# Seven unread matmuls instead of nine at the start, and at least two out matmuls behind each burst that holds values

## The chip, the cores and the metric

The kernel runs on one core of one Trainium2 chip. The metric is the device time of one execution in microseconds (us). A core has a matrix engine (PE in the profile; its weight loads stand apart as PEld), a vector engine (DVE), an activation engine (ACT), GpSimd (POOL) and a sync engine (SP). Matmuls write into eight banks of an accumulator memory, from where DVE and ACT read the results. The engines run by themselves and wait for each other by semaphores. Each takes its own instructions in the order in which the program has them, so an instruction that waits holds up everything behind it on its engine.

## The reference

Sigmoid attention over 8 batches, 12 heads, 448 positions and 64 channels, followed by a two-layer network with a SiLU in between:

```python
scores = scale * np.matmul(q, k.transpose(0, 1, 3, 2)) - np.log(S)
attn = 1.0 / (1.0 + np.exp(-scores))
x = np.matmul(attn, v)          # then heads side by side: 3584 rows of 768
h = x @ w_in                    # 768 -> 2048
g = h * (1.0 / (1.0 + np.exp(-h)))
out = g @ w_out                 # 2048 -> 768
```

There is no softmax: each score goes through a sigmoid by itself, so attention needs no sums over a row.

## The kernel before, in words

**Groups and tiles.** A group `g` is one batch with four heads (two pairs); there are 24, three to a batch. Each has seven score tiles. A tile (`scores`, L218) is four matmuls into one double bank `psc` (L225), which work beside each other in the four quarters of the array, and one ACT instruction (L232) that takes the sigmoid of all 896 columns and writes `attnT`. The values of a group (`values`, L240) are 28 matmuls (L256) into `pav`, behind which DVE scales two halves into `xT` (L267).

**Start.** The first q comes by two loads on the SP and ACT queues into a buffer `qs` and is cast to half precision by DVE (columns of the first four chunks, L629) and ACT (the rest, L630). The first two chunks of k come by a POOL load with a cast on the way (L617, L124). PE meanwhile runs `keep_busy(9)` (L675): matmuls of 512 columns on a constant, into a bank that nobody reads. Behind it, in PE's order, stand the first transposes (`pe_transpose`, L676 and L196): eight for the first part of q, two for chunk 0 of k, six for the rest of q, two for chunk 1 of k. DVE and ACT copy them out (L203, L186). The scores of tile 0 need all of q and chunk 0 of k. Then comes a list written by hand (`behind`, L698) of what PE does behind each of the tiles 0 to 23; in it `keep_busy(2)` stands behind tiles 2, 3, 6 and 7.

**Batches 0 and 1.** Bursts of two tiles (`burst`, L740) alternate with the first layer for these batches (`first_h`).

**Stretches m = 0, 1, 2.** Each computes attention for the next two batches (42 tiles) and fills PE with the second layer of the two batches before, the out matmuls of 384 columns (`sets`, `out_set`, L504). That layer is done as a Strassen-like product: seven products of eight matmuls each stand in for eight, with sums by DVE. The 42 tiles go in 18 bursts of 2, 2 and 3 tiles, six times over. A burst that finds a complete group waiting also runs that group's values (L745): a round is the seven tiles of a group, so from the second round on that is the first burst of each round, five in a stretch. In what follows **A** is this burst (two tiles and the values), **B** the next (two tiles), **C** the third (three tiles).

**How many out matmuls follow a burst** is planned (L774 to L789). The planner gives each burst a share of the stretch's PE time by its number of tiles, takes off what it reckons for the burst (200 ns, 200 ns a tile, 1330 ns for values) and fills the rest with out matmuls of 163 ns each, but at least one; the remainder goes on to the next burst. Worked through by its own numbers it gives, in m = 0 and m = 2, 9, 8 and 14 in the first round and then 1, 8 and 14 behind A, B and C of the other five. In m = 1, which has 56 out matmuls more, it gives 3 or 4 behind A, 11 or 12 behind B and 17 or 18 behind C. `rows_if_any` (L591), called behind each burst and again half way through its out matmuls, sends at most one sum and one copy to DVE, and a transposing load to SP.

**Accumulator banks in a stretch.** `banks_for_attention(3)` makes three double banks and two single ones. `two_banks` hands out the doubles in turn, to `psc` and, in these stretches, to `pav` too. So each use waits until the use three before it has been read. In the order A1, A2, values, B1, B2, C1, C2, C3 that is: B1 takes the bank of A1, B2 that of A2, C1 that of the values, C2 that of B1, C3 that of B2, and the next A1, A2 and values those of C1, C2 and C3. The single banks hold the products of the second layer in turn (`one_bank`).

Behind a stretch `h_pair` (L362) computes the first layer of its two batches, again as a Strassen-like product; after m = 2 the second layer of the last two batches ends the kernel.

Of the kernel before, what the change touches and what calls it, by code (L numbers as in the profile page):

```python
# [17 lines left out]
def kernel(  # L18
# [19 lines left out]
    NT_B = NQ * NCH  # L38
# [25 lines left out]
    def banks_for_attention(doubles):  # L64
        psum.close()
        banks.clear()
        bufs_of.update(double=doubles, single=NBANK - 2 * doubles)
        for name, bufs in bufs_of.items():
            taken[name] = 0
            new_pool(name, bufs)  # L70
# [7 lines left out]
    def banks_for_h():  # L78
        doubles = [[2 * i, 2 * i + 1] for i in longest_idle("double")]
        ring[:] = sum(doubles[:-2], [])  # L80
        ring.extend(2 * bufs_of["double"] + i for i in longest_idle("single"))
        ring.extend(sum(doubles[-2:], []))
        psum.close()
        banks.clear()
        new_pool("any", 1)
        for i in range(NBANK):
            banks[i] = banks["any"].tile([P, 512], F32, tag=f"any{i}", name=f"any{i}")

    def one_bank(name):
        if "any" in banks:  # L90
            ring.append(ring.pop(0))
            return banks["any"].tile([P, 512], F32, tag=f"any{ring[-1]}", name=name)
        taken["single"] += 1
        return banks["single"].tile([P, 512], F32, tag="single", name=name)
# [83 lines left out]
    def keep_busy(n):  # L178
        if n == 0:
            return  # L180
        pw = one_bank("pw")
        for _ in range(n):
            nc.tensor.matmul(pw, dummy[:, :P], dummy, start=True, stop=True)
# [4 lines left out]
    def pe_transpose(g, pieces=(("k", 0, 4), ("k", 4, NCH), ("q", 0, 4), ("q", 4, NCH))):  # L188
        if ("k", g) not in qkT:
            new_qkT(g)  # L190
        for name, c0, c1, *copy in pieces:
            dst = qkT[name, g].rearrange("p c t -> p (c t)")
            ptr = one_bank(f"ptr{name}")
            for c in range(c0, c1):
                for j in range(2):
                    nc.tensor.matmul(  # L196
                        ptr[j * D : (j + 1) * D, (c - c0) * P : (c - c0 + 1) * P],
                        flat[name, g][:, j, c, :],
                        ident,
                        start=True,  # L200
                        stop=True,
                    )
            (copy[0] if copy else nc.vector.tensor_copy)(  # L203
                dst[:, c0 * P : c1 * P], ptr[:, : (c1 - c0) * P]
            )
# [12 lines left out]
    def scores(g, ch):  # L218
        attnT[g, ch] = p12.tile([P, 2, S], F16, tag="attnT", name="attnT")
        psc = two_banks("psc")  # L220
        for half in range(2):
            own = slice(half * HP, (half + 1) * HP)
            for j in range(2):
                rows = slice(j * D, (j + 1) * D)
                nc.tensor.matmul(  # L225
                    psc[own, j, :S],
                    qkT["k", g][rows, ch, own],
                    qkT["q", g][rows, :, own],
                    start=True,
                    stop=True,  # L230
                )
        nc.scalar.activation(attnT[g, ch], psc[:, :, :S], AF.Sigmoid, bias=bias_s, scale=QKSCALE)  # L232
# [7 lines left out]
    def values(g, end=NCH):  # L240
        b, iq = divmod(g, NQ)
        if b not in xT:
            assert b < 2 or b - 2 in h_done
            xT[b] = p2.tile([P, NPAIR, S], F16, tag="xT", name="xT")
        pav, done_rounds = part_of.pop(g, None) or (None, 0)
        if pav is None and bufs_of["double"] > 2 and "any" not in banks:
            both = two_banks("pav")
            pav = [both[:, half] for half in range(2)]
        elif pav is None:
            pav = [one_bank("pav") for _ in range(2)]  # L250
        for ch in range(done_rounds, end):
            at = attnT.pop((g, ch))
            for half in range(2):
                own = slice(half * HP, (half + 1) * HP)
                for j in range(2):
                    nc.tensor.matmul(  # L256
                        pav[half][j * D : (j + 1) * D, :S],
                        flat["v", g][own, j, ch, :],
                        at[own, j, :],
                        start=(ch == 0),  # L260
                        stop=(ch == NCH - 1),
                    )
        if end < NCH:
            part_of[g] = pav, end
            return
        for half in range(2):
            nc.vector.tensor_scalar_mul(xT[b][:, half * NQ + iq, :], pav[half][:, :S], SX)  # L267
        if iq == NQ - 1:
            ready.add(b)
# [302 lines left out]
    def sets(m):  # L572
        for g in range(0, NCH - 1, 2):
            step = out_set(
                block(m, g), row_blocks(m, g), block(m, g + 1), row_blocks(m, g + 1)
            )
            for i, ns in enumerate(step):
                if m == 0 and g == 0 and i in (10, 14):
                    next(sums)
                if m == 0 and g == 0 and i in (20, 28, 36, 44):  # L580
                    next(in_sums)
                yield ns
        if m % 2 == 1:
            g = NCH - 1
            yield from out_set(
                kept, row_blocks(m - 1, g), block(m, g), row_blocks(m, g), m == B // 2 - 1
            )
# [3 lines left out]
    def rows_if_any(before, copy):  # L591
        if sums_of_x and next(sums_of_x[0], "end") == "end":
            sums_of_x.pop()
        if later and later[0][0] < before:
            g, name = later.pop(0)
            dma_transpose(g, name, copy)
            if name == "q":
                behind_rows(g, before)
# [68 lines left out]
    def values_if_any():  # L667
        if waiting:
            g = waiting.pop(0)
            values(g)  # L670
            after_values(g)
            return True
        return False

    keep_busy(9)  # L675
    pe_transpose(  # L676
        0, (("q", 0, SPLIT), ("k", 0, 1, act_copy), ("q", SPLIT, NCH, act_copy), ("k", 1, FIRST))
    )
# [61 lines left out]
    def burst(n, size=2):  # L740

        new = units[n : n + size]
        for u in new:
            scores(*u)
        with_values = values_if_any()  # L745
        for g, ch in new:
            if ch == NCH - 1:
                waiting.append(g)
                if 9 <= g + 3 < NQB:
                    later.extend(((g + 3, "k"), (g + 3, "q")))  # L750
        return with_values
# [14 lines left out]
    SWITCH, TILE, VALUES, DENSE = 200, 200, 1330, 163  # L766
    for m in range(B // 2 - 1):
        banks_for_attention(3)
        nc.scalar.activation(warm, bias_s, AF.Sigmoid)
        stream = sets(m)  # L770
        for _ in range(FIRST_DENSE):
            next(stream)

        dense = (3 + m % 2) * 7 * NHC - FIRST_DENSE - ENDING  # L774
        sizes = [2, 2, 3]
        costs = sum(SWITCH + TILE * size for size in sizes) * 2 * NQ + VALUES * (2 * NQ - 1)
        total = dense * DENSE + costs
        own = 2 * NQ * (m + 2)
        left, n = 0.0, 2 * NT_B * (m + 1)
        for size in sizes * (2 * NQ):  # L780
            left += total * size / (2 * NT_B) - SWITCH - TILE * size - VALUES * burst(n, size)
            n += size
            rows_if_any(own, nc.vector.tensor_copy)
            count = max(1, round(left / DENSE))
            left -= count * DENSE
            half = count // 2
            for i in range(count):
                next(stream)
                if i == half:  # L789
                    rows_if_any(own, nc.vector.tensor_copy)  # L790
        assert not sums_of_x
        nc.scalar.activation(warm, bias_s, AF.Silu)
        for _ in stream:
            pass
        (g,) = waiting
        waiting.clear()
        banks_for_h()

        def last_values():
            values(g)  # L800
            after_values(g)
            for _ in x_sums(m + 1, NQ - 1, NQ):
                pass
            nc.gpsimd.tensor_copy(gate, tx[m + 1, 4][:1, NQ - 1, :1])

        for i, _ in enumerate(h_pair(m + 1, last_values)):
            if i % 8 == 7:
                rows_if_any(NQB, nc.gpsimd.tensor_copy)
# [33 lines left out]
```

## Time and profile before

| | us |
|---|---|
| median of 3 runs | 369.35 (368.84 to 369.56) |
| the profiled execution's own time | 369.54 |
| its span, first to last instruction | 367.6 |
| PE busy in the span | 359.3 (98%) |
| DVE, ACT, POOL busy | 251.8 (69%), 250.0 (68%), 77.5 (21%) |

By stage, from a table of the profile by stretches of the span (busy us):

| stretch of the span | what | PE | ACT |
|---|---|---|---|
| 0 to 78 | batches 0 and 1 | 74.2 | 60.0 |
| 78 to 123 | m = 0 | 45.0 | 40.9 |
| 123 to 158 | first layer | 35.0 | 21.6 |
| 158 to 209 | m = 1 | 50.9 | 39.5 |
| 209 to 243 | first layer | 34.0 | 20.7 |
| 243 to 293 | m = 2 | 50.0 | 45.6 |
| 293 to 331 | first layer | 38.0 | 21.2 |
| 331 to 367.6 | last second layer | 32.2 | 0.5 |

The end of a matmul is modelled in these records, and a matmul's record lasts longer than the step to the next one, so a PE that is busy without a gap can still have waited for a while. Such waits are read from the starts. A line of the timeline has the start, the time covered, the engine, the line of the code, the operation, what it writes and reads, its shape and how many were put together; in brackets stands idle time of the engine before it and what ended that.

### The profile page before, as it was taken

The page shows a single profiled execution, that of the slowest core. Times are in us where ns is not written, and L with a number is a line of the kernel's source. Part 1 is how long each engine was busy: PE and PEld are TensorE (multiplying, and loading weights), DVE is VectorE, ACT ScalarE, POOL GpSimd, SP SyncE. Part 2 cuts the span into 40 slices and gives each one's busy share as a digit, 9 for nine tenths or more (in the row PEclk, how much of TensorE's full clock was granted, in tenths as well). Part 3 has the DMA queues.
Part 4 walks back from the last instruction along what each step waited for, and adds up shares of the span by engine and source line. Part 5 has one row for each costly group of instructions (what it writes and reads, how often), then busy time and mean ns, then how long its engine had stood idle before and what let it go on. Part 6 is the DMA issues. An engine that isn't in the chain of part 4 may idle for free. (4 is left out here: it accounts for less than half of the span.)

```text
span 367.6 us, 7594 instructions
## 1 busy us (share of the span) xinstructions
PE 359.3 (98%) x3009; PEld 183.8 (50%) x3009; DVE 251.8 (69%) x458; ACT 250.0 (68%) x339; POOL 77.5 (21%) x116
## 2 busy tenths in 40 slices
PE   7999999999999999999999999999999999999995
PEld 3554445545544555545445555554455555555552
DVE  2565559957756587867665768795756677797763
ACT  5998886479998756687777846679998956640000
POOL 8566521040061172000041047000100000000000
PEclk9999999999999999999999999999999999999999
DMA  8999999987989599007589359922863020003333
GB/s 132 198 204 202 204 203 204 197 115 134 153 114 223 117 135 177 2 0 162 92 168 206 61 128 129 135 24 51 151 113 86 19 71 0 3 0 86 87 86 85
DMA packets 65858, 42.78 MB, mean 116 GB/s; under 512 B 36128, under 2 KB 62496, under 8 KB 65824
## 3 DMA queue, kind: packets, MB, share of 16 engines
q0 software_dynamic: 27072, 22.58, 43.0%
q1 hardware_dynamic: 38320, 19.34, 27.0%
q8 instruction: 23, 0.38, 0.4%
q10 hardware_dynamic: 432, 0.39, 0.3%
q14 instruction: 11, 0.09, 0.1%
HBM read 45.61 MB, written 11.01 MB: 154 GB/s over the span
## 5 line engine op out<-in xcount | busy, mean ns | idle before, releaser
L232 ACT ACTIVATE attnT<-psc,bias_s 128x896 f16<-128x896 f32 x168 | 158.1, 1009 | 21.9 <-PE psc L225 21.6
L504 PEld LDWEIGHTS <-S 128*128 128x128 f16 x448 | 41.3, 98 | 36.5 <-issue 8.1
L225 PE MATMUL psc<-qT,kT 64*64 64x448 f16 x672 | 51.1, 362 | 1.4 <-DVE kT L203 0.5
L267 DVE TENSOR_SCALAR xT<-pav 128x448 f16<-128x448 f32 x48 | 27.7, 619 | 32.5 <-PE pav L256 32.5
L124 POOL DMA_DIRECT2D vf<-in_v_dram x24 | 17.3, 721 | 136.0 <-PE pav L256 118.1
L504 PEld LDWEIGHTS <-gTr 128*128 128x128 f16 x336 | 31.3, 98 | 26.6 <-issue 7.7
L504 PE MATMUL po<-T,S 128*128 128x384 f16 x224 | 42.0, 327 | 0.2
L504 PE MATMUL po<-w_out_sb,gTr 128*128 128x384 f16 x224 | 41.6, 327 | 0.0
L378 PEld LDWEIGHTS <-w_in_sb 128*128 128x128 f16 x288 | 27.9, 98 | 26.7 <-issue 1.1
L504 PE MATMUL po<-w_out_sb,S 128*128 128x384 f16 x224 | 40.8, 326 | 0.0
L256 PE MATMUL pav<-attnT,vf 64*64 64x448 f16 x672 | 38.3, 350 | 0.5 <-DVE gTr L303 0.4
L288 PE MATMUL ph<-xT,w_in_sb 128*128 128x448 f16 x192 | 38.7, 353 | 0.1
L378 PE MATMUL pa<-xT,w_in_sb 128*128 128x448 f16 x144 | 33.1, 353 | 0.0
L225 PEld LDWEIGHTS <-kT 64*64 64x64 f16 x672 | 17.8, 104 | 28.7 <-issue 22.3
L378 PEld LDWEIGHTS <-SI 128*128 128x128 f16 x216 | 21.1, 98 | 20.0 <-issue 0.5
L256 PEld LDWEIGHTS <-vf 64*64 64x64 f16 x672 | 21.0, 107 | 13.3 <-issue 3.8
L288 PEld LDWEIGHTS <-w_in_sb 128*128 128x128 f16 x192 | 17.8, 98 | 19.1 <-issue 3.7
L394 ACT ACTIVATE part<-pa 128x448 f32<-128x448 f32 x24 | 13.1, 544 | 19.2 <-PE pa L378 18.3
L504 PE MATMUL po<-T,gTr 128*128 128x384 f16 x112 | 22.1, 327 | 0.0
L372 ACT ACTIVATE gTr<-pc 128x448 f16<-128x448 f32 x24 | 13.1, 544 | 12.9 <-DVE pc L388 12.5
L388 DVE TENSOR_TENSOR part<-pb,part 128x448 f32<-128x448 f32 x24 | 14.9, 621 | 8.3 <-ACT part L394 5.0
L186 ACT ACTIVATE m<-po 128x384 f32<-128x384 f32 x1 | 0.5, 491 | 27.7 <-PE po L504 27.7
(75 smaller groups left out, 468.2 us busy)
## 6 DMA issues: line engine op xcount, KB each, us to landing
out_dram<-osb SPq DMA_DIRECT2D x52, 192.0 KB, 3.0
vf<-in_v_dram POOLq DMA_DIRECT2D x24, 224.0 KB, 6.5
kf<-in_k_dram POOLq DMA_DIRECT2D x23, 224.0 KB, 6.9
qf<-in_q_dram POOLq DMA_DIRECT2D x23, 224.0 KB, 7.4
w_in_sb<-in_moe_w_in_dram POOLq DMA_DIRECT2D x16, 192.0 KB, 8.1
w_out_sb<-in_moe_w_out_dram POOLq DMA_DIRECT2D x4, 768.0 KB, 14.9
out_dram<-osb SPq DMA_DIRECT2D x6, 96.0 KB, 2.1
kT<-kr SPq DMA_TRANSPOSE x18, 3.5
```

What stands on the lines that cost most here:

```text
L124: nc.gpsimd.dma_start(flat[name, g][:, :, c0:c1].rearrange("p i c d -> p i (c d)"), rows_in(name, g)[:, :, c0 * D : c1 * D],)
L186: nc.scalar.activation(o, i, AF.Copy)
L225: nc.tensor.matmul(psc[own, j, :S], qkT["k", g][rows, ch, own], qkT["q", g][rows, :, own], start=True, stop=True,)
L232: nc.scalar.activation(attnT[g, ch], psc[:, :, :S], AF.Sigmoid, bias=bias_s, scale=QKSCALE)
L256: nc.tensor.matmul(pav[half][j * D : (j + 1) * D, :S], flat["v", g][own, j, ch, :], at[own, j, :], start=(ch == 0), stop=(ch == NCH - 1),)
L267: nc.vector.tensor_scalar_mul(xT[b][:, half * NQ + iq, :], pav[half][:, :S], SX)
L288: nc.tensor.matmul(ph[:, :S], w_in_sb[:, cc, fc * P : (fc + 1) * P], xT[b][:, cc, :], start=(at == 0), stop=(at == NCC - 1),)
L372: nc.scalar.activation(gTr[:, r * NG + i, col + c * S : col + (c + 1) * S], h, AF.Silu, bias=0.0, scale=ISX)
L378: nc.tensor.matmul(to, w[:, n, i * P : (i + 1) * P], x[:, n], start=(start and n == 0), skip_group_check=not start, stop=(n == NQ - 1),)
L388: nc.vector.tensor_add(o, po, x)
L394: nc.scalar.activation(got[i, 1], bank[i, "a"], AF.Copy)
L504: nc.tensor.matmul(po[:, :NO2], a[:, fc, :], w[:, fc, :], start=(fc == 0), stop=(fc == NHC - 1))
```

## The change

```diff
-    keep_busy(9)
+    keep_busy(7)
     pe_transpose(
         0, (("q", 0, SPLIT), ("k", 0, 1, act_copy), ("q", SPLIT, NCH, act_copy), ("k", 1, FIRST))
     )
...
         for size in sizes * (2 * NQ):
-            left += total * size / (2 * NT_B) - SWITCH - TILE * size - VALUES * burst(n, size)
+            with_values = burst(n, size)
+            left += total * size / (2 * NT_B) - SWITCH - TILE * size - VALUES * with_values
             n += size
             rows_if_any(own, nc.vector.tensor_copy)
-            count = max(1, round(left / DENSE))
+            count = max(1 + with_values, round(left / DENSE))
             left -= count * DENSE
             half = count // 2
```

Two of the nine unread matmuls ahead of the first transposes go. In the stretches, the least number of out matmuls behind a burst with values rises from one to two. Worked through, the counts behind A, B and C become 2, 7 and 14 instead of 1, 8 and 14 in the five rounds with values of m = 0 and m = 2; m = 1, with 3 or 4 behind A, stays as it is. So in ten places one out matmul moves from behind burst B to ahead of it. The instructions of DVE, ACT, POOL and SP and their order on these engines stay the same, and PE's lose the two matmuls and their two weight loads.

## The prediction

> **What bounds the kernel now.** I read the busy shares first (PE 98%), then the table by stretches, because both parts of the change sit in single stages.
>
> ```profile
> 78.00:123.00 45.00, 45.00 (x465) 22.76 (x464) 32.10 (x60) 40.89 (x45) 8.83 (x14) 1.00 0.97 147
> 243.00:293.00 50.00, 50.00 (x493) 25.43 (x491) 33.97 (x62) 45.59 (x51) 2.15 (x3) 1.00 0.40 74
> ```
>
> The columns after the length are PE, PEld, DVE, ACT and POOL. In the stretches m = 0 and m = 2 PE has no gap, so whatever lengthens its order there lengthens the kernel; but ACT is at 91% as well, so PE may be waiting on ACT inside its "busy" time. For that I read PE's timeline of one round of m = 0 (A, values, out, B, out, C, out) and ACT's beside it.
>
> ```profile
> 92.69 0.57 PE L225 MATMUL psc<-qT,kT 64*64 64x448 f16 x8
> 93.09 1.49 PE L256 MATMUL pav<-attnT,vf 64*64 64x448 f16 x28
> 94.51 0.34 PE L504 MATMUL po<-w_out_sb,gTr 128*128 128x384 f16 x1
> 94.78 0.74 PE L225 MATMUL psc<-qT,kT 64*64 64x448 f16 x8
> 95.45 0.66 PE L504 MATMUL po<-w_out_sb,gTr 128*128 128x384 f16 x3
> 95.95 0.98 PE L504 MATMUL po<-T,S 128*128 128x384 f16 x5
> 96.86 0.76 PE L225 MATMUL psc<-qT,kT 64*64 64x448 f16 x12
> 97.55 1.96 PE L504 MATMUL po<-T,S 128*128 128x384 f16 x11
> ```
>
> ```profile
> 93.18 1.91 ACT L232 ACTIVATE attnT<-psc,bias_s 128x896 f16<-128x896 f32 x2 [0.27 <-PE psc L225]
> 95.28 1.91 ACT L232 ACTIVATE attnT<-psc,bias_s 128x896 f16<-128x896 f32 x2 [0.19 <-PE psc L225]
> 97.35 2.81 ACT L232 ACTIVATE attnT<-psc,bias_s 128x896 f16<-128x896 f32 x3 [0.17 <-PE psc L225]
> ```
>
> The same eight score matmuls cover 0.57 us in A and 0.74 us in B. So B's second tile waits about 0.17 us. It needs the bank of A2, whose sigmoid ends at 93.18 + 1.91 = 95.09; a narrow window there has it starting 0.05 us later:
>
> ```profile
> 95.14 0.38 PE L225 MATMUL psc<-qT,kT 64*64 64x448 f16 x4
> ```
>
> This wait is what an out matmul moved ahead of B would fill. The next question is what comes late then. C's third tile needs the bank of B2. It starts here:
>
> ```profile
> 97.26 0.36 PE L225 MATMUL psc<-qT,kT 64*64 64x448 f16 x4
> ```
>
> B2's sigmoid ends at 95.28 + 1.91 = 97.19, plus 0.05 is 97.24: C3 escapes by 0.02 us. In the first round with values of m = 2 it does not escape: C's twelve matmuls cover 0.82 us instead of 0.76, and their third tile starts at 259.67.
>
> ```profile
> 259.23 0.82 PE L225 MATMUL psc<-qT,kT 64*64 64x448 f16 x12
> ```
>
> So the loop from B1 over two sigmoids to C3 is already at its limit. For the start I read PE's first lines and the landing of the first piece of k.
>
> ```profile
> 1.46 4.02 PE L183 MATMUL pw<-dummy 128*128 128x512 f16 x9 [1.46 <-DVE bias_s L627]
> 5.41 0.64 PE L196 MATMUL ptrq<-ident,qf 128*64 128x128 f16 x8
> 5.84 0.31 PE L196 MATMUL ptrk<-ident,kf 128*64 128x128 f16 x2
> 5.94 0.47 PE L196 MATMUL ptrq<-ident,qf 128*64 128x128 f16 x6
> ...
> 7.00 0.57 PE L225 MATMUL psc<-qT,kT 64*64 64x448 f16 x8 [0.53 <-DVE kT L203]
> ...
> 8.81 0.60 PE L183 MATMUL pw<-dummy 128*128 128x512 f16 x2
> ```
>
> ```profile
> kf<-in_k_dram POOLq DMA_DIRECT2D x1, 64.0 KB, 4.1
> ```
>
> The nine unread matmuls start 0.43 us apart (their weight loads stand at 1.86, 2.29, 2.72 and so on), but the pair at 8.81 only about 0.22. PE therefore runs at about half speed until some time after 5.4 us, and at full speed by 8.8.
>
> **Part 1, the start: −0.35 us.** Two matmuls less take 2 × 0.43 = 0.85 us out ahead of the transposes, which could then start at 5.41 − 0.85 = 4.56. Their q is there: DVE's cast ends at 3.98 + 0.43 = 4.41, ACT's at 4.20 + 0.52 = 4.72, and the eight transposes take until 4.98. What is late next is k. Its first piece was issued at 1.24 on POOL's queue, which the change doesn't touch, and landed 4.1 us later, at 5.35. The transposes of k, now at 5.84, can start 0.02 to 0.1 us behind that (DVE's cast started 0.02 us behind its load), so at 5.4: at most 0.45 us is won, and the other 0.4 become a wait for k. The six transposes of q behind them run wholly at half speed then, where the last ones now run faster as the clock rises: some 0.05 us goes back. I take 0.35; the ends are 0 (k lands later in some executions) and 0.45.
>
> The first sigmoid then starts at 7.08 instead of 7.43, and ACT, 0.89 us a tile without a gap until about 26 us, carries this on. The tightest load behind it is q of group 3, transposed at 18.80 and landed 0.5 us before; 0.35 fits.
>
> **Part 2, ten rounds: +0.16 us each, +1.60 us.** All is in PE's starts, relative to the out matmul at 94.51.
>
> Now: one out matmul takes 0.27 to B1 (94.78 − 94.51); B with its wait 0.67 (95.45 − 94.78); eight out matmuls 1.41; C 0.69. From the first out matmul to the one behind C: 97.55 − 94.51 = 3.04.
>
> After, PE's work alone: an out matmul takes 0.163 in a row, and m = 1 shows three behind values taking 0.59 to B1 (178.10 to 178.69), so two take 0.43. B without a wait takes 0.51 (178.69 to 179.20, the same pair in m = 1). Seven take 1.41 − 0.16 = 1.25, C 0.69. That is 2.88, and 0.17 would be won.
>
> But C3 waits for B2's sigmoid. From B1's start to ACT's start is 0.50 (95.28 − 94.78), two sigmoids 1.91, release to matmul 0.05: 2.46 from B1 to C3. The round of m = 2 with the wait measures just that, 259.67 − 257.21 = 2.46. PE's own work in between is only 0.51 + 1.25 + 0.21 + 0.19 (C1 and C2) = 2.16. So C3 stands 0.30 us, and starts 0.43 + 2.46 = 2.89 behind the first out matmul, where it is 97.26 − 94.51 = 2.75 now: 0.14 later. A tile that has waited also takes 0.32 to the next matmul where one in a row takes 0.29 (both by starts, B's last and C's last), so C gives 0.02 more: +0.16.
>
> In words: B1, which starts the loop over ACT, moves back by one out matmul, and the loop can't be made shorter by taking work out of it. ACT has no cover: the 0.17 us that it now idles ahead of C goes, and 0.16 more appears ahead of B. B2's old wait is gone (its bank is free at 95.14, it is reached at 95.15), but it was hidden under this loop already. Next A: its banks and the values' are C1's to C3's, whose sigmoids end before PE's 14 out matmuls do, so nothing is won back there. DVE has the same order; product ends move by 0.1 to 0.2 us against its 0.6 us operations, with single banks a whole product (1.3 us) apart, so I cost it at nothing; 0.1 us a round if that fails. The ends for a round: +0.10 and +0.17, and, if the loop weren't there, −0.17.
>
> No stage between has PE idle, so all of it reaches the end. **Sum:** +1.60 − 0.35 = +1.25 on 369.54, so 370.8 for an execution like the profiled one. That one stands 0.19 above the median of 369.35, on which the forecast is **370.6**.
>
> **Rivals.**
>
> *The wait goes and nothing takes its place (0.13).* For it: B2's wait is real and one out matmul fills it exactly. Against: C3's margin of 0.02 us. It decides if C3's bank comes free 0.3 us sooner than I reckon, for instance if ACT took B1 up earlier. Then each round wins 0.17: −1.70 − 0.35 = −2.05, 367.3.
>
> *The two waits balance (0.15).* For it: rounds are bound by the loop of ACT either way, and if B1 was also late for another reason, its delay may be absorbed ahead of C or A. Against: A and C show no other waits. Part 2 gives 0, the start −0.35: 369.0.
>
> *The clock comes late (0.17).* Full speed came at about 6.2 us (transposes stand 0.107 us apart until then), after 4.8 us in which PE hardly paused. After the change PE works 3.5 us, waits 0.4 for k, works 0.5 and waits for the copies. If that restarts the count, a further 4.8 us from 5.4 ends at 10.2, and some three tiles run at half speed. A tile with its pair of unread matmuls then takes about 2 × (0.21 + 0.43) = 1.28 instead of ACT's 0.89: 0.39 each, 1.2 in all, and 0.1 on the first scores: 370.6 + 1.3 = 371.9. Against: the half-speed time before had a pause too, at its end. The Trainium skill (TensorE: Matmul & The Clock Gate, Part 1) speaks for this rival: about 3.4 us of sustained work in a window that runs freely release the clock, and seven matmuls last 3.0 where nine last 3.8. The trace's 4.8 us agree with such a window met part way; by the page one lost window would be some two tiles, 371.4.
>
> *That the change does less than it says* can be read off: the new least count binds only where the old one gave 1, in m = 0 and 2, ten times.
>
> **Numbers.** The forecast has 0.55, on its own 370.2 (a round at +0.13, the start at 0.45) to 371.1 (+0.17, nothing at the start). The range takes in the balance and the late clock and leaves out the first rival: 368.8 to 372.0. This kernel's runs tell about 0.2% (0.7 us) from no change. Slower by more: forecast and late clock, 0.72; within: the balance, 0.15; faster: 0.13.
>
> **What would show it.** In m = 0 and 2 of the changed profile: two out matmuls behind values, 0.43 us to B1; B's eight matmuls back at 0.57; C's twelve at 1.05 to 1.1 instead of 0.76, with C3 0.05 us behind a sigmoid's end; rounds of 7.41 us where they are 7.25 (94.51 to 101.76). C at 0.76 would prove me wrong. At the start: the first transposes at 4.6, those of k at 5.4 after a wait, the first scores at 6.65; transposes of k at 5.0 would mean that k came sooner. Unread matmuls 0.43 apart behind tile 2 would show the late clock.

## The result, and the profile after

The changed kernel takes 370.79 us (median of 7 runs; 370.67 for the six that the ratio takes in) where the kernel before takes 369.47 (median of 7): the ratio is 1.0034, 95% interval 1.0024 to 1.0044, so 0.34% slower. One of the seven executions, the one that was profiled there, took 724 us and is left out of the ratio: from its first matmul to its last the steps between matmuls are longer (0.39 us between most out matmuls instead of 0.163, 0.417 between those of the first layer instead of 0.190), though its granted clock is shown as 1.000. The profile after is that of a second set of six runs of the same kernel (median 371.18, ratio 1.0048, 1.0034 to 1.0062). Its profiled execution took 370.41 us, with a span of 368.4.

PE's timeline of one round of m = 0 in the changed kernel, which answers to the one of before:

```profile
92.17 0.57 PE L225 MATMUL psc<-qT,kT 64*64 64x448 f16 x8
92.57 1.49 PE L256 MATMUL pav<-attnT,vf 64*64 64x448 f16 x28
94.00 0.50 PE L504 MATMUL po<-w_out_sb,gTr 128*128 128x384 f16 x2
94.42 0.58 PE L225 MATMUL psc<-qT,kT 64*64 64x448 f16 x8
94.94 0.50 PE L504 MATMUL po<-w_out_sb,gTr 128*128 128x384 f16 x2
95.27 0.98 PE L504 MATMUL po<-T,S 128*128 128x384 f16 x5
96.18 1.09 PE L225 MATMUL psc<-qT,kT 64*64 64x448 f16 x12
97.19 1.96 PE L504 MATMUL po<-T,S 128*128 128x384 f16 x11
```

and ACT's beside it:

```profile
92.66 1.91 ACT L232 ACTIVATE attnT<-psc,bias_s 128x896 f16<-128x896 f32 x2 [0.54 <-PE psc L225]
94.92 4.60 ACT L232 ACTIVATE attnT<-psc,bias_s 128x896 f16<-128x896 f32 x5 [0.35 <-PE psc L225]
```

Two out matmuls stand behind the values, and B's eight score matmuls cover 0.58 us instead of 0.74: its old wait is gone. C's twelve cover 1.09 instead of 0.76. Its third tile, seen alone in a narrow window, starts 96.88 − 94.42 = 2.46 us behind B1:

```profile
96.88 0.38 PE L225 MATMUL psc<-qT,kT 64*64 64x448 f16 x4
```

Its bank is that of B2, whose sigmoid ends at 95.83 + 1.00 = 96.83, so it starts 0.05 us behind that end:

```profile
95.83 1.00 ACT L232 ACTIVATE attnT<-psc,bias_s 128x896 f16<-128x896 f32 x1
```

On ACT the five sigmoids of B and C now form one block without a gap, so the 0.17 us of idle time ahead of C has gone, and the idle time has grown from 0.19 to 0.35 us ahead of B and from 0.27 to 0.54 ahead of A. The next round's out matmuls start at 101.40: a round takes 7.40 us where it took 7.25.

By stages (from the first score matmul of a stage, or its first `pa` matmul, to the next such start):

| us | first scores at | to m = 0 | m = 0 | first layer | m = 1 | first layer | m = 2 | rest | span |
|---|---|---|---|---|---|---|---|---|---|
| before | 7.00 | 71.34 | 44.68 | 35.78 | 53.31 | 35.78 | 44.81 | 74.87 | 367.58 |
| after | 6.16 | 71.51 | 45.45 | 35.78 | 53.32 | 35.78 | 45.58 | 74.88 | 368.45 |

m = 0 and m = 2 are 0.77 us longer each. The start is 0.84 us earlier in this execution and 0.17 of that is lost before m = 0. Everything else is the same to 0.01 us. That is 0.77 + 0.77 − 0.84 + 0.17 = +0.87, as much as the spans differ by.

The start of the changed kernel:

```profile
1.46 3.06 PE L183 MATMUL pw<-dummy 128*128 128x512 f16 x7 [1.46 <-DVE bias_s L627]
4.45 0.41 PE L196 MATMUL ptrq<-ident,qf 128*64 128x128 f16 x8
5.16 0.25 PE L196 MATMUL ptrk<-ident,kf 128*64 128x128 f16 x2 [0.29 <-DMA kf<-in_k_dram]
5.24 0.33 PE L196 MATMUL ptrq<-ident,qf 128*64 128x128 f16 x6
...
6.16 0.57 PE L225 MATMUL psc<-qT,kT 64*64 64x448 f16 x8 [0.53 <-ACT qT L186]
```

The transposes of k do wait for k's load, as forecast. But here the eight transposes of q cover 0.41 us, not 0.64: full speed had come by 4.5 us, which is luck of this execution, as the runs below show.

### The profile page after: what moved, and what is told of

It is laid out like the page before. It is cut to its first block, busy times and chain, and to the rows that moved or that the text cites. A ratio compares the mean times of both kernels' runs of the same rounds, so it can differ in the third digit from the quotient of the medians.

```text
span 722.0 us, 7590 instructions
## 1 busy us (share of the span) xinstructions
PE 715.6 (99%) x3007; PEld 261.6 (36%) x3007; DVE 258.9 (36%) x458; ACT 254.6 (35%) x339; POOL 77.5 (11%) x116
## 4 chain that ended last, share of the span: by engine, by line
PE 99%; DVE 0%; ACT 0%; issue 0%
PE po L504 38%; PE ph L288 11%; PE psc L225 10%; PE pav L256 10%; PE pc L378 8%; PE pa L378 8%; PE pd L378 8%; PE pb L378 4%; PE pw L183 1%; PE ptrk L196 1%; PE ptrq L196 1%; DVE osb L541 0%; ACT qT L186 0%; DVE dummy L626 0%; DVE kT L203 0%
## 5 line engine op out<-in xcount | busy, mean ns | idle before, releaser
L504 PE MATMUL po<-T,S 128*128 128x384 f16 x224 | 82.4, 552 | 0.0
L504 PE MATMUL po<-w_out_sb,S 128*128 128x384 f16 x224 | 82.3, 556 | 0.0
L504 PE MATMUL po<-w_out_sb,gTr 128*128 128x384 f16 x224 | 82.3, 550 | 0.0
L288 PE MATMUL ph<-xT,w_in_sb 128*128 128x448 f16 x192 | 79.2, 610 | 0.0
L225 PE MATMUL psc<-qT,kT 64*64 64x448 f16 x672 | 77.9, 559 | 0.7 <-ACT qT L186 0.4
L256 PE MATMUL pav<-attnT,vf 64*64 64x448 f16 x672 | 74.8, 618 | 0.0
L378 PE MATMUL pa<-xT,w_in_sb 128*128 128x448 f16 x144 | 66.2, 615 | 0.0
L124 POOL DMA_DIRECT2D vf<-in_v_dram x24 | 17.2, 716 | 387.1 <-PE pav L256 386.0
L378 PE MATMUL pc<-tx,w_in_sb 128*128 128x448 f16 x72 | 34.7, 632 | 0.0
L378 PE MATMUL pc<-xT,w_in_sb 128*128 128x448 f16 x72 | 34.6, 623 | 0.0
L378 PE MATMUL pd<-tx,SI 128*128 128x448 f16 x72 | 34.5, 623 | 0.0
```

Source lines behind the costliest of these rows:

```text
L124: nc.gpsimd.dma_start(flat[name, g][:, :, c0:c1].rearrange("p i c d -> p i (c d)"), rows_in(name, g)[:, :, c0 * D : c1 * D],)
L225: nc.tensor.matmul(psc[own, j, :S], qkT["k", g][rows, ch, own], qkT["q", g][rows, :, own], start=True, stop=True,)
L256: nc.tensor.matmul(pav[half][j * D : (j + 1) * D, :S], flat["v", g][own, j, ch, :], at[own, j, :], start=(ch == 0), stop=(ch == NCH - 1),)
L288: nc.tensor.matmul(ph[:, :S], w_in_sb[:, cc, fc * P : (fc + 1) * P], xT[b][:, cc, :], start=(at == 0), stop=(at == NCC - 1),)
L378: nc.tensor.matmul(to, w[:, n, i * P : (i + 1) * P], x[:, n], start=(start and n == 0), skip_group_check=not start, stop=(n == NQ - 1),)
L504: nc.tensor.matmul(po[:, :NO2], a[:, fc, :], w[:, fc, :], start=(fc == 0), stop=(fc == NHC - 1))
```

## The experiments

Each was timed in five rounds beside the kernel before, on one chip with the others of its batch. The medians of before in the three batches are 369.52, 369.58 and 369.62 us.

**The changed kernel again** (the profile above).

> The changed kernel once more, for a profile at full clock. Theory (the loop from B1 over two sigmoids to C3, 2.46 us, is the limit): +1.25 us against before, rounds of m = 0 and m = 2 at 7.41 us instead of 7.25, B's eight score matmuls covering 0.57 us instead of 0.74, C's twelve 1.05 to 1.1 instead of 0.76. Rival (the clock comes late and the rounds cost nothing): rounds at 7.25 or less, and unread matmuls 0.43 us apart behind tile 2.

Ratio 1.0048 (1.0034 to 1.0062), so +1.8 us; by medians 371.18 against 369.52. Rounds, B and C are as the theory of the loop has them. The unread matmuls behind tile 2 run at full speed in this execution.

**Seven unread matmuls alone.**

```diff
-    keep_busy(9)
+    keep_busy(7)
```

> Seven unread matmuls at the start, the old least count of one out matmul. Theory: -0.35 us against before (0 to -0.45), because the transposes of k wait for its load. Rival (late clock): +0.5 to +1.3 us, with half-speed matmuls behind tile 2.

The median is 369.19 us, 0.33 below before, but the ratio is 1.0003 (0.9988 to 1.0019): the twelve runs lie from 368.64 to 371.39, seven of them up to 369.25 and four from 370.11 on, where the 23 of before end at 370.30. The profile is of one of these four (370.12 us):

```profile
1.46 3.17 PE L183 MATMUL pw<-dummy 128*128 128x512 f16 x7 [1.46 <-DVE bias_s L627]
4.56 0.64 PE L196 MATMUL ptrq<-ident,qf 128*64 128x128 f16 x8
5.43 0.32 PE L196 MATMUL ptrk<-ident,kf 128*64 128x128 f16 x2 [0.23 <-DMA kf<-in_k_dram]
...
6.65 0.96 PE L225 MATMUL psc<-qT,kT 64*64 64x448 f16 x8 [0.47 <-ACT qT L186]
...
9.01 1.04 PE L183 MATMUL pw<-dummy 128*128 128x512 f16 x2
...
10.29 0.60 PE L183 MATMUL pw<-dummy 128*128 128x512 f16 x2
```

Its first scores start at 6.65, 0.35 earlier than in the profile of before, as worked out. But eight score matmuls take 0.96 instead of 0.57, and the pair of unread matmuls at 9.01 takes 1.04, that at 10.29 only 0.60: full speed came at about 9.9 us. From the first scores to m = 0 this execution takes 72.23 us instead of 71.34. So the rival holds in this execution. The seven runs up to 369.25 are as short as the theory has them, or shorter; none of them was profiled.

**At least two out matmuls behind values, alone.**

```diff
-            left += total * size / (2 * NT_B) - SWITCH - TILE * size - VALUES * burst(n, size)
+            with_values = burst(n, size)
+            left += total * size / (2 * NT_B) - SWITCH - TILE * size - VALUES * with_values
...
-            count = max(1, round(left / DENSE))
+            count = max(1 + with_values, round(left / DENSE))
```

> Nine unread matmuls at the start, at least two out matmuls behind values (2, 7, 14 in ten rounds). Theory of the loop: +1.6 us against before, +0.16 a round, with C's third tile 0.05 us behind the end of B2's sigmoid. Rival (the wait of B2 goes and nothing takes its place): -1.7 us.

370.66 us, ratio 1.0042 (1.0029 to 1.0055), so +1.6 us. m = 0 takes 45.45 and m = 2 45.57 us: 0.77 and 0.76 more. The rival is out.

**Two behind values, the second one taken from behind C** (counts 2, 8, 13).

```diff
             left -= count * DENSE
+            if m % 2 == 0 and n > 2 * NT_B * (m + 1) + 7:
+                at = (n - 2 * NT_B * (m + 1)) % 7
+                count += {2: 1, 4: 0, 0: -1}[at]
```

> As before with nine unread matmuls, but the second out matmul behind values is taken from behind C instead of B: 2, 8, 13 in the ten rounds. Theory of the loop: B1 to C3 is still 2.46 us, of which PE's own work is now 2.32, so C3 waits 0.14 us instead of 0.30 and one out matmul less follows: rounds of 7.24 us, 0 against before (within 0.2 us). Rival (an out matmul more behind values costs 0.16 us a round wherever it is taken from, because B1 starts later): +1.6 us. Rival (only the wait of B2 mattered): -1.7 us.

369.40 us, ratio 1.0004 (0.9996 to 1.0013): no change. m = 0 takes 44.65, m = 2 44.77 us (before: 44.68, 44.81). C's third tile waits half as long as after the change: its twelve matmuls cover 0.92 us.

```profile
94.82 0.58 PE L225 MATMUL psc<-qT,kT 64*64 64x448 f16 x8
95.33 0.50 PE L504 MATMUL po<-w_out_sb,gTr 128*128 128x384 f16 x2
95.67 1.14 PE L504 MATMUL po<-T,S 128*128 128x384 f16 x6
96.73 0.92 PE L225 MATMUL psc<-qT,kT 64*64 64x448 f16 x12
```

So B may start an out matmul later at no cost; what costs is taking that matmul from inside the loop B1 to C3, where it was hidden under ACT's two sigmoids.

**Eight unread matmuls.**

```diff
-    keep_busy(9)
+    keep_busy(8)
```

> Eight unread matmuls at the start, least count of one. Theory (what is won is set by the landing of k, and the spread by how long PE works without a pause): k has landed when the q transposes end at 5.4, so PE doesn't pause; -0.3 us or so against before in the median, and the runs spread no wider than those of before (1.5 us). Rival (each unread matmul taken out is worth 0.43 us, and spread has nothing to do with the start): -0.43, and -0.85 for seven.

369.31 us against 369.58, 0.27 less; ratio 0.9994 (0.9986 to 1.0003). The eleven runs spread over 1.0 us, as those of before do (1.1). In the profile k's transposes follow those of q without a gap, and the first scores start at 6.51. The rival's 0.43 for one is not seen, though it lies inside the interval (down to −0.5); its 0.85 for seven is not what the profile of `start_only` shows, where the wait for k leaves 0.35.

**Seven, and one more ahead of k's transposes.**

```diff
-    keep_busy(9)
...
+    fill(7)
+    pe_transpose(0, (("q", 0, SPLIT),))
+    fill(1)
+    pe_transpose(0, (("k", 0, 1, act_copy), ("q", SPLIT, NCH, act_copy), ("k", 1, FIRST)))
```

(`fill` issues the same unread matmul as `keep_busy`.)

> Seven unread matmuls, then the first eight q transposes, then one more unread matmul, where seven alone leave PE waiting for k. Theory (the pause of 0.4 us is what lets the full clock come late): the first scores start as early as with seven, but no run comes out above 370.5, as some did with seven alone: -0.35 us in the median. Rival (the wide spread of seven has another cause): runs up to 371.4 as with seven alone.

369.20 us, 0.38 less; ratio 0.9998 (0.9989 to 1.0008). Ten of twelve runs end at 369.46, but two came out at 370.34 and 370.51. The late ones became fewer and milder (seven alone: four, up to 371.39), and did not go away as expected. Filling the wait helps or does nothing; twelve runs don't settle it. Nor would they tell the filled wait from the number: this kernel has eight unread matmuls, as `start_8` has, none of whose eleven runs was above 369.81.

**Five unread matmuls.**

```diff
-    keep_busy(9)
+    keep_busy(5)
```

> Five unread matmuls: PE pauses from 3.7 to 4.45 for the cast of q and again for k. Theory of the late clock: full speed comes late in nearly all executions; median +0.5 to +2 us against before, although the first transposes still start at 4.5. Rival (only the landing of q and k counts): as with seven, -0.35 us.

371.08 us, ratio 1.0038 (1.0025 to 1.0052), so +1.4 us. Five of the six runs are at 370.86 or above. In the profile (of the sixth, 369.69 us) the first scores start at 6.16 and still run at half speed, until about 9.7 us:

```profile
1.46 2.31 PE L183 MATMUL pw<-dummy 128*128 128x512 f16 x5 [1.46 <-DVE bias_s L627]
4.36 0.64 PE L196 MATMUL ptrq<-ident,qf 128*64 128x128 f16 x8 [0.59 <-DVE qf L629]
...
6.16 0.96 PE L225 MATMUL psc<-qT,kT 64*64 64x448 f16 x8 [0.48 <-ACT qT L186]
```

From its first scores to m = 0 it takes 72.31 us instead of 71.34. Here the unread matmuls that are left out cost by the clock: the first scores come 0.84 us sooner than in the profile of before, and the whole is no shorter. That the clock also made the other five runs long is argued from their times, since none was profiled.

**Other counts: 5, 10, 11 in the first round, then 2, 9, 13.**

```diff
             left -= count * DENSE
+            if m % 2 == 0:
+                at = (n - 2 * NT_B * (m + 1)) % 7
+                first = n <= 2 * NT_B * (m + 1) + 7
+                count = {2: 5, 4: 10, 0: 11}[at] if first else {2: 2, 4: 9, 0: 13}[at]
```

> Nine unread matmuls; the counts of m = 0 and m = 2 set by hand to 5, 10, 11 in the first round and 2, 9, 13 in the other five: five out matmuls go from the first round to the others. Theory of the loop: with nine behind B, PE's own work from B1 to C3 is 2.48 us, just over the loop's 2.46, and B2's wait goes too; about -0.1 us a round, less 0.1 to 0.3 a stretch for the shorter first round: -0.5 a stretch, -1.0 us against before. Rival (rounds are bound by ACT as a whole, so no choice of counts wins): 0.

368.53 us against 369.58, ratio 0.9971 (0.9960 to 0.9982), so −1.1 us, where −1.0 was worked out. m = 0 takes 44.25 and m = 2 44.21 us. B covers 0.57 us and C 0.77: neither waits.

```profile
94.12 0.50 PE L504 MATMUL po<-w_out_sb,gTr 128*128 128x384 f16 x2
94.55 0.57 PE L225 MATMUL psc<-qT,kT 64*64 64x448 f16 x8
95.05 1.15 PE L504 MATMUL po<-w_out_sb,gTr 128*128 128x384 f16 x6
96.03 0.65 PE L504 MATMUL po<-T,S 128*128 128x384 f16 x3
96.62 0.77 PE L225 MATMUL psc<-qT,kT 64*64 64x448 f16 x12
```

**These counts with eight unread matmuls, and the order of loads.** The second kernel also moves one load on POOL's queue:

```diff
-    load("v", 2)
...
         if g == 0:
             load("kq", 3)
+            load("v", 2)
```

> The counts 5, 10, 11 and 2, 9, 13 together with eight unread matmuls. If the two add up: -1.05 - 0.25 = -1.3 us against before. If the start is limited by the loads of group 3 (they landed 0.04 us before their transposes in the profiles with an early start): -1.1 to -1.3.

> The same, with the load of v of group 2 behind the loads of k and q of group 3 on POOL's queue instead of ahead of them. Theory (the start's gain is cut off by the landing of k and q of group 3 at 17.2 and 18.3 us): these land about 1.1 us sooner, their transposes no longer wait, and 0.1 to 0.3 us more is won where the clock comes early. Rival (the next load in the queue, or v of group 2 itself, is the limit): no change against eight with the counts alone.

368.21 us, ratio 0.9964 (0.9950 to 0.9977), and 367.93, ratio 0.9958 (0.9945 to 0.9970). In the first, the transposes of group 3 wait for their loads:

```profile
17.84 0.58 PE L196 MATMUL ptrk<-ident,kf 128*64 128x128 f16 x14 [0.20 <-DMA kf<-in_k_dram]
...
18.93 0.58 PE L196 MATMUL ptrq<-ident,qf 128*64 128x128 f16 x14 [0.20 <-DMA qf<-in_q_dram]
```

In the second they start at 17.36 and 18.18 without a wait, and the stretch from the first scores to m = 0 takes 71.34 us, as in the profile of before, instead of 71.64. The medians differ by 0.28 us, which the intervals alone would not tell from nothing; stage and wait agree with the theory. By medians this version is 1.7 us faster than the kernel before, where the changed kernel is 1.2 to 1.7 us slower.

## Why the prediction was right, point by point

**The sum.** Forecast +1.25 us; measured in the two sets +1.2 (over the six runs) and +1.7 by medians, and +1.3 and +1.8 by the ratios. That the first set meets the forecast to 0.1 us is in part luck: part 2 came out at +1.54 in the profile, and of the 0.35 that the start was to give back the mean of seven alone shows nothing (ratio 1.0003).

**Part 2, +0.16 us a round.** Right in mechanism and in size. B1 to C3 measures 2.46 us, the figure worked out; rounds measure 7.40 (7.41 was given), C 1.09 (1.05 to 1.1), and a stretch +0.77 where five rounds at 0.16 make +0.80. What carried it was the question what comes late next: the margin of 0.02 us at C3 was in the profile of before, and the one round of m = 2 that had no margin showed the loop's length. The first two rivals failed on this row: the wait of B2 (0.17 us) went, and a longer one at C3 (0.33 us by what C covers) took its place, where the first rival has none and the second no longer one. `from_c` and `counts` show the same loop from two sides: it costs when work leaves it, and nothing when work is taken from elsewhere.

**Part 1, −0.35 us.** The mechanism was right: the transposes of k wait for the load in both profiles with seven, and the first scores start 0.35 us sooner in that of `start_only`, the size that was worked out. As a mean it is not seen: the ratio for seven alone is 1.0003, though its interval still holds −0.35 us; and the changed kernel, at +1.2 and +1.7 us by medians, is not faster than `floor_only`, which has nine and the second part alone, at +1.1. The step that failed is the single time at which full speed comes, and with it the third rival, which was put into a case of its own with a chance of 0.17, as if an execution of the kernel either had it or not at all. It comes to some executions and not to others. In the profile of `start_only` it costs 72.23 − 71.34 = 0.89 us, where the rival was priced at 1.3; that of the fastest run of `start_5` has it too. That the other three runs of `start_only` over 370.1 us and the five longer ones of `start_5` had it is argued from their times alone.

What I had as one fixed time, full speed at 6.2 us, moves from run to run. In the seven profiles with nine or eight unread matmuls it came between 4.1 and 6.2 us (first scores at 6.25 to 7.00), in two of the four with fewer at 9.7 and 9.9. The Trainium skill (TensorE: Matmul & The Clock Gate, Part 1) has the clock released by a window of 3.4 us that runs freely, so that the number of slow matmuls differs from run to run. The profiles are in keeping with that: the early rises spread over 2.1 us, and the late ones come 3.5 and 3.7 us behind the last of them, about one window. What makes an execution miss its window is not shown. A pause within it fits `start_5` and `start_only`, but with fewer unread matmuls PE pauses more and runs fewer matmuls of 512 columns at once, and no run tells the two apart. Why some runs of seven took 371.4, 1.3 us more than the profiled late one, was not profiled and stays open; a second missed window would be one reading.

**No stage between has PE idle, so all of it reaches the end.** Right for part 2. For the start it is limited by the loads of group 3, for whose q a margin of 0.5 us was named. That margin moves from run to run: k and q of group 3 landed at 17.2 and 18.3 us in the profile of before and at about 17.8 and 18.9 in that of `counts_8`, where they ended waits of PE and 0.30 us was lost before m = 0, although the first scores had come only 0.41 us sooner. In three of the four profiles whose first scores came at 6.16 to 6.25 the loads of group 3, and in one of them that of q of group 1 as well, ended waits of PE, and 0.17 us or more of the earlier start was lost before m = 0 (71.51 instead of 71.34 after the change); the fourth, `start_5`, lost more by its late clock. `counts_8_v2`, which brings these loads forward, has its 71.34 back.

**DVE at nothing.** Right as far as the profile shows: five rounds of 0.15 to 0.16 us make up the whole 0.77 us of a stretch, so nothing is left for DVE, and no wait for a product's bank appeared in m = 0 and m = 2.

## What to carry to other kernels

When a wait is to be filled with work that is moved, look at where the work comes from: here it came from inside a loop (scores, sigmoid, bank free, scores) that was already as long as the wait on its far side allowed, and the wait came back longer. A wait of 0.17 us that a profile shows is not a gain of 0.17 us: lay down the whole round with the releases of every bank, and find the margin of the next one. For unread matmuls that keep the clock up, compare the spread of many runs and not one profile.

## What the runs showed of the hardware that was not expected

Nine unread matmuls and seven can give nearly the same start (first scores at 6.25 us in `counts`, at 6.16 in the changed kernel), since full speed came as early as 4.1 us (2.7 us after the first matmul) and as late as 9.9. The first score matmuls of kernels with nine started at 6.25, 6.53, 6.88 and 7.00 us: a spread of 0.75 us with the same instructions at the start, where full speed came at 4.2, 5.0, 5.8 and 6.2 us and the first piece of k landed at about 5.0 to 5.4.
